# A fused attention and two-FFN kernel: the first stage's instructions put in an order written as a string, and x split by one operation per engine and tile

## The chip, the core and the metric

The kernel runs on one core of a Trainium2 chip. The metric is the device time of one execution in microseconds (us). The engines of the core are PE (matrix products, with its weight loads shown apart as PEld), DVE (vector), ACT (scalar functions), POOL (a second, slower vector engine) and SP, whose queue issues all the DMA transfers. Each engine takes its instructions strictly in the order in which the program has them; an instruction that waits holds up everything behind it on its engine.

## The reference, cut to what matters

```python
# q, k, v: (4, 8, 576, 64); chunks of 64 rows attend within themselves
scores = matmul(q_c, k_c.T) / 8
attn = exp(scores - max(scores)); attn /= sum(attn) + 1e-9
x = matmul(attn, v_c)  -> transposed to (2304, 512)
# first FFN: w_in (512, 2048), w_out (2048, 512), float64 in memory
h = x @ w_in
x = (h - tanh(h)) @ w_out
# second FFN: 8 experts (512 -> 1024 -> 512), weighted by a normalised gate
P = softmax-like matrix (2304, 8), rows and columns normalised 8 times
out = sum_e P[:, e:e+1] * (maximum(x @ w1[e], 0) @ w2[e])
```

## The kernel before

The 2304 tokens are 18 attention tiles of 128 rows (128 rows hold two chunks, and all 8 heads lie beside each other in 512 columns), and 6 blocks of 384 tokens for the FFNs; three tiles make a block. Every operand of an FFN product is kept as a high and a low part, and a product of two such operands is three PE products (`mm3`).

One attention tile T goes through: loads of q, k and v (three DMAs of 256 KB); four PE transposes each of q and k, copied out of PSUM by ACT (`stage_a`, L253 and L255); 16 small products for the scores into the one PSUM tile `s` (L265), then on DVE the row maximum and the subtraction (L268, L270) and on ACT the exponential (L271); the sum, the reciprocal and the scaling of the rows (`stage_b2`, L277 to L281: DVE for the first four tiles, then POOL scales); four transposes of the result, copied to the one tile `at` (`stage_c`, L288, L290); and 16 products with v into the one PSUM tile `x` (L300), which is split into x_hi (ACT, L307) and x_lo (DVE, L308), half a tile at a time (`stage_d`).

The first FFN is done in slots. Slot i makes one 128x384 piece of h from x and a quarter of w_in (12 PE products, L320, "h"; `layer1`), sends it through a polynomial and tanh on ACT, DVE and POOL in the slots that follow (`act_1`, `act_2`, `act_3a`, `act_3b`), and makes one piece of the second product, of a slot that is six back (12 PE products, L320, "y"; `layer2_ffn1`), which DVE adds to an accumulator (L398). 24 slots use one quarter of the weights; there are 96. The weights come from memory as 64-bit floats: `split64` takes a 128x512 piece apart with DVE bit operations (L160, L161), two ACT operations (L166, L167), two DVE operations (L169, L170), a POOL product (L171), and a high and a low part (ACT L174, POOL L175). 16 pieces are taken apart before slot 30.

In the stretch in which attention runs, the program emits its stages round by round (`ROUNDS`, `ROUND`), and a scheduler of the language then orders the instructions of each engine by its own rules. From `ctx.enter_context(tc.manual_schedule())` on, behind the last attention tile, the order is that of the code, slot by slot. What the second FFN does, behind slot 96, is written out by hand as well.

Of the kernel before, what the change touches and what calls it, by code (L numbers as in the profile page):

```python
# [8 lines left out]
F32 = mybir.dt.float32  # L9
# [3 lines left out]
ALU = mybir.AluOpType  # L13
# [14 lines left out]
def block_attention_two_ffn_kernel(ctx, tc, q, k, v, w_in, w_out, w_gate, w1, w2, out):  # L28
# [123 lines left out]
    def split64(key):  # L152

        which, u, c = key
        t = raws.pop(key).bitcast(U32).rearrange("p (n two) -> p n two", two=2)
        lw, hw = t[:, :, 0], t[:, :, 1]
        e = cvp.tile([P, 512], F32, tag="cve", name="cve")
        m = cvp.tile([P, 512], F32, tag="cvm", name="cvm", bufs=2)
        eu, mu = e.bitcast(U32), m.bitcast(U32)
        nc.vector.tensor_scalar(eu, hw, 20, 0x7FF, ALU.logical_shift_right, ALU.bitwise_and)  # L160
        nc.vector.tensor_scalar(mu, hw, 0xFFFFF, None, ALU.bitwise_and)  # L161
        if cvq:
            ep, mp = cvq[0].tile([P, 512], F32, tag="cvq", name="cvq"), pgp[0].tile([P, 512], F32, tag="sm", name="cvs")
# [12 lines left out]
        (w1t if which == "a" else w2t)[u, c] = (hi, lo)
# [16 lines left out]
    def do_load(n=1):  # L193
        for _ in range(n):
            if nload[0] < len(order):
                load_raw(order[nload[0]])
                nload[0] += 1

    running = []

    def split_step():

        if not running and nsplit[0] < NS64:
            running.append(split64(order[nsplit[0]]))
            nsplit[0] += 1
        if running:
            try:
                next(running[0])
            except StopIteration:
                running.pop()  # L210
                do_load()

    def early_step(n=1):
        for _ in range(n):
            if nsplit[0] < 10 or running:
                split_step()

    def next_raw(which, k):
        if k < NU2:
# [24 lines left out]
            )  # L244
        st[T][nm] = t

    def stage_a(T):
        r = st[T]
        for nm in ("q", "k"):
            pt = ps.tile([P, NP, P], F32, tag="t", name="t", bufs=2)  # L250
            src = r.pop(nm).rearrange("p (n two) d -> p n (two d)", two=2)
            for p in range(NP):
                nc.tensor.transpose(pt[:, p, :], src[:, p, :], ident)  # L253
            r[nm + "t"] = t = ap_.tile([P, NP, P], F32, tag=nm + "t", name=nm + "t")
            nc.scalar.copy(t, pt)  # L255

    def stage_b(T):
        r = st[T]
        qt, kt = r.pop("qt"), r.pop("kt")
        sp = ps.tile([P, NP, 2, CH], F32, tag="s", name="s")  # L260
        for p in range(NP):
            for c in range(2):
                for h in range(2):
                    hs, cs = slice(h * D, (h + 1) * D), slice(c * CH, (c + 1) * CH)
                    nc.tensor.matmul(sp[hs, p, c, :], qt[hs, p, cs], kt[hs, p, cs], start=True, stop=True)  # L265
        s3 = sp.rearrange("p n c j -> p (n c) j")
        mx = ap_.tile([P, 2 * NP], F32, tag="mx", name="mx")
        nc.vector.tensor_reduce(mx, s3, AX.X, ALU.max)  # L268
        ex = ap_.tile([P, 2 * NP, CH], F32, tag="ex", name="ex", bufs=3)
        nc.vector.tensor_tensor(ex, s3, mx.unsqueeze(2).to_broadcast([P, 2 * NP, CH]), ALU.subtract)  # L270
        nc.scalar.activation(ex, ex, AF.Exp, scale=1.0 / float(D) ** 0.5)  # L271
        r["ex"] = ex

    def stage_b2(T):
        ex = st[T]["ex"]
        sm = ap_.tile([P, 2 * NP], F32, tag="sm", name="sm")
        nc.vector.tensor_reduce(sm, ex, AX.X, ALU.add)  # L277
        nc.vector.tensor_scalar(sm, sm, EPS, None, ALU.add)
        nc.vector.reciprocal(sm, sm)
        eng = nc.vector if T < 4 else nc.gpsimd  # L280
        eng.tensor_tensor(ex, ex, sm.unsqueeze(2).to_broadcast([P, 2 * NP, CH]), ALU.mult)  # L281

    def stage_c(T):
        r = st[T]
        ex = r.pop("ex").rearrange("p (n c) j -> p n (c j)", c=2)
        pt = ps.tile([P, NP, P], F32, tag="t", name="t", bufs=2)
        for p in range(NP):
            nc.tensor.transpose(pt[:, p, :], ex[:, p, :], ident)  # L288
        r["at"] = at = ap_.tile([P, NP, P], F32, tag="at", name="at", bufs=1)
        nc.scalar.copy(at, pt)  # L290

    def stage_d(T):
        r = st.pop(T)
        at, vt = r["at"], r["v"]
        px = ps.tile([P, 2, 512], F32, tag="x", name="x")
        for p in range(NP):
            for c in range(2):
                for h in range(2):
                    hs, cs = slice(h * D, (h + 1) * D), slice(c * CH, (c + 1) * CH)
                    nc.tensor.matmul(  # L300
                        px[hs, c, p * CH:(p + 1) * CH], vt[cs, 2 * p + h, :], at[cs, p, hs], start=True, stop=True
                    )
        b, t = divmod(T, TT)
        for c in range(2):
            o = slice(t * P + c * CH, t * P + (c + 1) * CH)
            src = px[:, c, :NP * CH].rearrange("p (n i) -> p n i", n=NP)
            nc.scalar.copy(x_hi[b][:, :, o], src)  # L307
            nc.vector.tensor_tensor(x_lo[b][:, :, o], src, f(x_hi[b][:, :, o]), ALU.subtract)  # L308


    acc = {}
# [35 lines left out]
    def act_1(i, ph):  # L347
        z = tmp.tile([P, TB], F32, tag="z", name="z")
        t = tmp.tile([P, TB], F32, tag="t", name="t", bufs=2)
        s1 = tmp.tile([P, TB], F32, tag="s1", name="s1")  # L350
        if s2p:
            s2 = s2p[0].tile([P, 512], F32, tag="s2", name="s2p")[:, :TB]
        else:
            s2 = tmp.tile([P, TB], F32, tag="s2", name="s2", bufs=2)
# [710 lines left out]
        return i // SPU, i % SPU // 4, i % 4  # L1065

    nsteps = {}
    for r in range(6):
        nsteps[SPU - 6 + r] = nsteps[SPU + r] = 1 + (r % 2)
    for r in range(SPU + 6, NS1 - SPU + 6):  # L1070
        nsteps[r] = 2 if r == SPU + 21 else 1

# [10 lines left out]
    todo = {}  # L1083

    def slot(i):
        u, b, c = at(i)
        while u == 0 and ((u, c) not in w1t or i >= LAG and (u, 3) not in w2t):
            split_step()
        ph = layer1(*at(i))
        if nsteps.get(i, 0) > 1:  # L1090
            split_step()
# [7 lines left out]

    PRE = early
    ROUNDS = ("BAb", "BEAbE", "DCBbEAE", "ABbE")
    ROUND = "DCBSEbASE"
    stages = {"A": stage_a, "B": stage_b, "b": stage_b2, "C": stage_c, "D": stage_d}
    before = {"B": "A", "b": "B", "C": "b", "D": "C"}
    done = dict.fromkeys(stages, 0)
    i = r = 0
    load(0, "q", q)
    load(0, "k", k)  # L1110
    while done["D"] < NTILE:
        if r + 1 < NTILE:
            load(r + 1, "q", q)
            load(r + 1, "k", k)
        if 1 <= r <= NTILE:
            load(r - 1, "v", v)
        if r < 2:
            do_load()
        goal = r - 3 if r < 7 else r - 4 if r < 10 else r * 4 // 3 - 8
        for op in ROUNDS[r] if r < len(ROUNDS) else ROUND:  # L1120
            if op == "E":
                early_step()
            elif op == "S":
                if i < min(PRE, goal, 4 * (done["D"] // TT)):
                    slot(i)
                    i += 1
            elif done[op] < (done[before[op]] if op in before else min(NTILE, r + 1)):
                stages[op](done[op])
                done[op] += 1
        r += 1  # L1130
    assert i <= PRE
    actx.close()
    yx = ExitStack()
    for r in rings:
        if r.more:
            r.extend(first=r not in (php, pyp), within=yx if r is pyp else ctx)
    accp += [pool(f"acc{b}") for b in range(4, NB)]
    pgp.append(yx.enter_context(tc.tile_pool(name="pgp", bufs=1, space=PSUM)))
    s2x = ExitStack()
    s2p.append(s2x.enter_context(tc.tile_pool(name="s2p", bufs=1, space=PSUM)))  # L1140
    cvq.append(s2x.enter_context(tc.tile_pool(name="cvq", bufs=1, space=PSUM)))
    ctx.enter_context(tc.manual_schedule())
    last = NS1 - SPU
    put = lambda r, task: todo.setdefault(last + r, []).append(task)
    put(0, gate_load)
# [114 lines left out]
```

## Time and profile before

| | us |
|---|---|
| median of three timed runs | 1978.49 |
| lowest and highest of them | 1977.0, 1979.21 |
| the profiled execution: its own time | 1978.26 |
| the profiled execution: span from first to last instruction | 1976.5 |
| busy in the span: PE, DVE, POOL, ACT | 1938.1, 1576.1, 1399.5, 918.7 |

The busy time of PE is made of pipelined instructions, so that 98% of the span says that PE rarely stands, not that its every instruction is at its best. The change touches the first 220 us or so; behind them the two programs do the same.

### The profile page before, as it was taken

Reading aid. Unit: us, or ns where it says so; the run is one execution under the profiler, and the core shown is the slowest. Engines: PE = TensorE matmul, PEld = TensorE weight load, DVE = VectorE, ACT = ScalarE, POOL = GpSimd, SP = SyncE. Lnnn points to the kernel's source line nnn. Section 1 sums busy time; section 2 is a strip of 40 time slices with the busy share of each in tenths; the row PEclk is TensorE's granted clock in tenths of the full one; section 3 lists DMA queues with packets and bytes.
Section 4 is the critical chain, followed back from the end, with each engine's and each line's share of the span. In section 5 each row is a group of like instructions: output and inputs, shape, how many; then the busy total and the mean of one; then the engine's idle time right before and its main releaser. Section 6 shows DMA issues by size and latency. Waiting matters only on the chain.

```text
span 1976.5 us, 35597 instructions
## 1 busy us (share of the span) xinstructions
PE 1938.1 (98%) x11708; PEld 1853.5 (94%) x11708; DVE 1576.1 (80%) x2599; ACT 918.7 (46%) x2095; POOL 1399.5 (71%) x1419
## 2 busy tenths in 40 slices
PE   7899999999999999999999999999999999999999
PEld 5799999999888889898889999999999999999998
DVE  7987888777689887778876888888877887777777
ACT  6766777766544655555543223222234233232222
POOL 3645677667566766667757888878778887777775
PEclk9899999999999999999999999999999999999999
DMA  8631111110498788888889888888888867988883
GB/s 182 149 82 38 54 44 44 43 33 22 148 316 287 274 302 303 301 296 303 313 287 348 259 262 260 262 261 252 262 258 260 260 212 264 314 261 262 261 252 118
DMA packets 307702, 430.51 MB, mean 218 GB/s; under 512 B 81696, under 2 KB 135232, under 8 KB 307520
## 3 DMA queue, kind: packets, MB, share of 16 engines
q1 hardware_dynamic: 307520, 428.25, 66.9%
q8 instruction: 94, 1.54, 0.3%
q14 instruction: 88, 0.72, 0.1%
HBM read 304.89 MB, written 123.26 MB: 217 GB/s over the span
## 4 chain that ended last, share of the span: by engine, by line
PE 78%; DVE 5%; ACT 1%; issue 1%; DMA 1%; POOL 1%; SPq 0%; DVEq 0%; POOLq 0%; ACTq 0%
PE h L592 33%; PE y L751 23%; PE y L320 16%; PE h L320 5%; DVE gl L600 1%; DVE acc L628 0%; DVE cvm L441 0%; DVE x L628 0%; DVE s L517 0%; ACT gh L599 0%; DMA raw<-in_moe_w 0%; DVE pm L1033 0%; DMA w1d<-wa 0%; DMA wb<-in_moe_w 0%; PE y L990 0%
## 5 line engine op out<-in xcount | busy, mean ns | idle before, releaser
L592 PE MATMUL h<-x,wa 128*128 128x384 f32 x4032 | 792.0, 337 | 1.6 <-DVE t L657 1.3
L592 PEld LDWEIGHTS h<-x,wa 128*128 128x128 f32 x4032 | 707.9, 188 | 13.7 <-DVE t L657 1.6
L751 PE MATMUL y<-gh,wb 128*128 128x384 f32 x1764 | 521.5, 336 | 0.6 <-issue 0.2
L756 DVE TENSOR_TENSOR acc<-y,acc 128x768 f32<-128x768 f32 x367 | 349.1, 954 | 135.7 <-PE y L751 135.1
L180 POOL TENSOR_TENSOR gl<-cvm,gh 128x384 fp32r<-128x384 f32 x252 | 264.6, 1050 | 133.7 <-ACT gh L179 133.7
L751 PEld LDWEIGHTS y<-gh,wb 128*128 128x128 f32 x1764 | 325.2, 188 | 2.4 <-ACT gh L179 1.5
L751 PE MATMUL y<-gl,wb 128*128 128x384 f32 x882 | 296.4, 336 | 0.0
L179 ACT CAST gh<-cvm 128x384 fp32r<-128x384 f32 x252 | 129.8, 515 | 288.7 <-DVE cvm L796 162.3
L179 ACT CAST gh<-z 128x384 fp32r<-128x384 f32 x189 | 97.4, 515 | 352.1 <-POOL z L812 226.6
L320 PE MATMUL y<-wb,gh 128*128 128x512 f32 x776 | 243.5, 395 | 0.0
L180 POOL TENSOR_TENSOR gl<-z,gh 128x384 fp32r<-128x384 f32 x189 | 199.7, 1056 | 45.6 <-ACT gh L179 41.2
L320 PE MATMUL h<-x,wa 128*128 128x384 f32 x1152 | 222.0, 340 | 5.9 <-DVE s L375 5.9
L320 PE MATMUL y<-gh,wb 128*128 128x384 f32 x768 | 214.1, 340 | 4.8 <-POOL wb L175 2.6
L320 PEld LDWEIGHTS h<-x,wa 128*128 128x128 f32 x1152 | 200.1, 189 | 9.6 <-DVE s L375 8.4
L320 PEld LDWEIGHTS y<-wb,gh 128*128 128x128 f32 x776 | 143.9, 188 | 26.0 <-issue 0.4
L751 PEld LDWEIGHTS y<-gl,wb 128*128 128x128 f32 x882 | 165.8, 188 | 0.0
L366 POOL TENSOR_TENSOR s<-s,s 128x384 f32<-128x384 f32 x96 | 99.1, 1033 | 82.4 <-DVE s L365 74.0
L320 PE MATMUL y<-wb,gl 128*128 128x512 f32 x388 | 152.9, 394 | 0.0
L180 POOL TENSOR_TENSOR wa<-cvm,wa 128x256 fp32r<-128x256 f32 x128 | 100.0, 781 | 73.4 <-ACT wa L179 70.9
L320 PEld LDWEIGHTS y<-gh,wb 128*128 128x128 f32 x768 | 141.3, 189 | 8.1 <-POOL wb L175 3.4
L599 ACT ACTIVATE gh<-h 128x384 fp32r<-128x384 f32 x99 | 48.7, 492 | 190.9 <-DVE h L688 96.2
L320 PE MATMUL y<-gl,wb 128*128 128x384 f32 x384 | 129.6, 338 | 0.0
(208 smaller groups left out, 3233.9 us busy)
## 6 DMA issues: line engine op xcount, KB each, us to landing
wa<-w1d SPq DMA_DIRECT2D x448, 256.0 KB, 3.2
wb<-w2d SPq DMA_DIRECT2D x441, 256.0 KB, 3.3
w1d<-wa SPq DMA_DIRECT2D x224, 256.0 KB, 2.7
w2d<-wb SPq DMA_DIRECT2D x192, 256.0 KB, 4.2
raw<-in_moe_w SPq DMA_DIRECT2D x33, 512.0 KB, 4.5
wb<-in_moe_w SPq DMA_DIRECT2D x62, 256.0 KB, 5.0
raw<-in_moe_w_in SPq DMA_DIRECT2D x16, 512.0 KB, 3.8
raw<-in_moe_w_out SPq DMA_DIRECT2D x16, 512.0 KB, 3.8
```

The lines of the kernel that those rows point to most:

```text
L179: nc.scalar.copy(hi, src)
L180: nc.gpsimd.tensor_tensor(lo, src, f(hi), ALU.subtract)
L320: nc.tensor.matmul(ps, lhsT, rhs, start=(i == 0), stop=(i == n - 1))
L366: nc.gpsimd.tensor_tensor(s1, s1, w, ALU.mult)
L592: nc.tensor.matmul(ps, w[:, a, kk, :], b[:, kk, :], start=(i < 3 and kk == 0 and s == 0), stop=(kk == 1 and s == 2), skip_group_check=(i > ...
L599: nc.scalar.activation(hi, src, AF.Relu)
L600: nc.vector.scalar_tensor_tensor(lo, src, 0.0, f(hi), ALU.max, ALU.subtract)
L751: nc.tensor.matmul(y[:, c, :], w[:, a, c, :], b, start=(s == 0), stop=(s == 2))
L756: nc.vector.tensor_tensor(m, y, m, ALU.add)
```

## The change

The scheduler is switched off from the first attention tile on. The stages are cut into 17 kinds of pieces, each a letter, with four more letters for the loads, and a string of 433 letters (`ORDER`) gives the order in which the program emits them; the n-th occurrence of a letter is the n-th tile, weight piece or slot. 1, 2 and 3 load q, k and v, 0 loads a raw weight piece; Q and K are the transposes, S the scores, B maximum, subtraction and exponential, R the row sums and scaling, C the transposes of the result, D the products with v, X the split of x; c, d and e are the three parts of taking a weight piece apart; l is the h product of a slot, z, y, x and w are the four parts of its activation, and m the y product. The string ends where slot 29 would have ended, with 30 l, 24 m and 16 weight pieces done. Behind it the program goes on with slot 30 as before.

The split of x is now one operation of 128x512 on each of ACT and DVE in place of two of 128x256. No other instruction is added or left out.

```diff
+ORDER = (
+    "2110KQ2Q1c1S2KBQdS01KR2BceCS3R0KBDdXQeR23CSQKD3BcR2SXC1dKD0X2QCe1cl3210B3KSzdQRBlyReDxXC2zS1QBKcyRl3",
...
-    def stage_a(T):
+    def turn(T, nm):
...
-        b, t = divmod(T, TT)
-        for c in range(2):
-            o = slice(t * P + c * CH, t * P + (c + 1) * CH)
-            src = px[:, c, :NP * CH].rearrange("p (n i) -> p n i", n=NP)
-            nc.scalar.copy(x_hi[b][:, :, o], src)
-            nc.vector.tensor_tensor(x_lo[b][:, :, o], src, f(x_hi[b][:, :, o]), ALU.subtract)
+    def split_x(T):
+        px = st.pop(T)["x"]
+        b, t = divmod(T, TT)
+        o = slice(t * P, (t + 1) * P)
+        src = px[:, :, :NP * CH].rearrange("p c (n i) -> p c n i", n=NP)
+        hi, lo = (x[b][:, :, o].rearrange("p n (c i) -> p c n i", c=2) for x in (x_hi, x_lo))
+        nc.scalar.copy(hi, src)
+        nc.vector.tensor_tensor(lo, src, f(hi), ALU.subtract)
...
-    for r in range(6):
-        nsteps[SPU - 6 + r] = nsteps[SPU + r] = 1 + (r % 2)
...
+    stages = {
+        "1": lambda T: load(T, "q", q), "2": lambda T: load(T, "k", k), "3": lambda T: load(T, "v", v),
+        "0": lambda j: do_load(),
+        "Q": lambda T: turn(T, "q"), "K": lambda T: turn(T, "k"), "S": scores, "B": soft_a, "R": soft_b,
+        "C": turn_ex, "D": times_v, "X": split_x,
+        "c": lambda j: split_begin(), "d": lambda j: next(running[dn[0] - en[0]]), "e": lambda j: split_end(),
+        "l": lambda i: ph_of.update({i: layer1(*at(i))}), "z": act_0, "y": act_2, "x": act_3a,
+        "w": lambda i: act_3b(i, at(i)), "m": lambda i: layer2_ffn1(*at(i)),
+    }
...
+    for op in "".join(ORDER):
+        stages[op](done[op])
+        done[op] += 1
+        dn[0], en[0] = done["d"], done["e"]
+        if op == "X" and done[op] == NTILE:
+            end_attention()
```

The first place is PE ahead of the first h product. In the names, t is a transposed tile, s the scores, x the product with v, and h the piece of slot 0. Before:

```order
18 L253 MATMUL t<-ident,q 128x128 x4
19 L300 MATMUL x<-at,v 64x64 x16
20 L253 MATMUL t<-ident,k 128x128 x4
21 L288 MATMUL t<-ident,ex 128x128 x4
22 L265 MATMUL s<-kt,qt 64x64 x16
23 L300 MATMUL x<-at,v 64x64 x13
24 L253 MATMUL t<-ident,q 128x128 x4
25 L300 MATMUL x<-at,v 64x64 x3
26 L253 MATMUL t<-ident,k 128x128 x4
27 L288 MATMUL t<-ident,ex 128x128 x4
28 L265 MATMUL s<-kt,qt 64x64 x16
29 L320 MATMUL h_635<-x,wa_329 128x384 x2
```

Now:

```order
16 L269 MATMUL t<-ident,k 128x128 x4
17 L318 MATMUL x<-at,v 64x64 x16
18 L281 MATMUL s<-kt,qt 64x64 x16
19 L306 MATMUL t<-ident,ex 128x128 x4
20 L269 MATMUL t<-ident,k 128x128 x4
21 L318 MATMUL x<-at,v 64x64 x16
22 L269 MATMUL t<-ident,q 128x128 x4
23 L306 MATMUL t<-ident,ex 128x128 x4
24 L341 MATMUL h_592<-x,wa_338 128x384 x2
```

Before, the scheduler cut the 16 products with v into pieces around other work; now each piece stands whole. Ahead of the first h product both programs have six transposes of q and of k, four of the result and three products with v; before there are six score products, now five.

The second place is DVE around the first splits of x (the destination x is a part of x_lo). Before:

```order
21 L268 TENSOR_REDUCE mx<-s 128x8
22 L160 TENSOR_SCALAR cve<-raw 128x512
23 L270 TENSOR_TENSOR ex<-s,mx 128x512
24 L308 TENSOR_TENSOR x<-x 128x4x64
25 L161 TENSOR_SCALAR cvm<-raw 128x512
26 L170 SCALAR_TENSOR_TENSOR cve<-raw,cve 128x512
27 L277 TENSOR_REDUCE sm<-ex 128x8
28 L308 TENSOR_TENSOR x<-x 128x4x64
29 L278 TENSOR_SCALAR sm<-sm 128x8
```

Now:

```order
21 L178 SCALAR_TENSOR_TENSOR cvm<-raw,cvm 128x512
22 L179 SCALAR_TENSOR_TENSOR cve<-raw,cve 128x512
23 L329 TENSOR_TENSOR x<-x 128x2x4x64
24 L295 TENSOR_REDUCE sm<-ex 128x8
25 L296 TENSOR_SCALAR sm<-sm 128x8
26 L297 RECIPROCAL sm<-sm 128x8
27 L299 TENSOR_TENSOR ex<-ex,sm 128x512
28 L287 TENSOR_REDUCE mx<-s 128x8
29 L289 TENSOR_TENSOR ex<-s,mx 128x512
```

Two rows of a tile have become one, and the operations of a piece stand together, where before those of two or three pieces were mixed.

## Rows read from the trace of the kernel before

**Rows 1.** PE by time around slot 0, slot 18 and slot 29's end (start, us).
```profile
37.44 0.80 PE L320 MATMUL h<-x,wa 128*128 128x384 f32 x3
...
164.20 2.35 PE L320 MATMUL h<-x,wa 128*128 128x384 f32 x12
...
218.96 0.34 PE L320 MATMUL y<-gh,wb 128*128 128x384 f32 x1
```

**Rows 2.** Busy by stretch: PE, PEld, DVE, ACT, POOL, granted clock, DMA share, GB/s.
```profile
0.00:9.35 9.35, 5.00 (x44) 3.93 (x44) 0.00 (x0) 2.46 (x3) 0.70 (x6) 1.00 0.95 197
9.35:164.20 154.85, 134.75 (x1689) 119.19 (x1686) 130.72 (x250) 109.10 (x239) 76.35 (x68) 0.96 0.54 122
164.20:219.20 55.00, 51.23 (x294) 49.72 (x288) 44.44 (x79) 39.14 (x87) 35.91 (x32) 1.00 0.16 49
220.10:400.00 179.90, 179.32 (x1031) 178.58 (x1032) 146.41 (x277) 135.14 (x304) 126.76 (x117) 1.00 0.15 45
400.00:1976.00 1576.00, 1567.72 (x8663) 1502.11 (x8661) 1253.59 (x1994) 632.24 (x1462) 1159.34 (x1198) 1.00 0.76 253
```

**Rows 3.** PE by time in a steady round of one tile and one slot.
```profile
126.33 0.69 PE L300 MATMUL x<-at,v 64*64 64x64 f32 x32
...
127.54 1.15 PE L265 MATMUL s<-kt,qt 64*64 64x64 f32 x32
128.62 2.35 PE L320 MATMUL h<-x,wa 128*128 128x384 f32 x12
...
132.89 0.60 PE L253 MATMUL t<-ident,q 128*128 128x128 f32 x4
...
133.86 0.69 PE L300 MATMUL x<-at,v 64*64 64x64 f32 x32
```

**Rows 4.** Busy by stretch again, inside the attention stretch.
```profile
9.35:111.00 101.65, 83.69 (x1095) 71.74 (x1093) 91.73 (x172) 73.36 (x158) 53.51 (x46) 0.95 0.69 157
...
37.44:68.00 30.56, 26.88 (x376) 23.27 (x374) 30.01 (x58) 26.35 (x59) 18.97 (x17) 1.00 0.72 172
```

**Rows 5.** What PE waited for, 30 to 220 us: total, times, longest.
```profile
PE h L320 <- DVE s L375: 3.8, 4, 1.4
PE x L300 <- DVE x L308: 3.6, 3, 2.0
PE s L265 <- ACT kt L255: 3.0, 3, 1.5
```

**Rows 6.** PE by time around a long wait.
```profile
71.09 0.45 PE L300 MATMUL x<-at,v 64*64 64x64 f32 x14 [1.99 <-DVE x L308]
...
73.28 1.98 PE L265 MATMUL s<-kt,qt 64*64 64x64 f32 x32
```

**Rows 7.** DVE by line and shape, first 164.2 us: busy us, mean ns, idle.
```profile
L365 DVE SCALAR_TENSOR_TENSOR s<-s,z 128x384 f32<-128x384 f32 x18 | 16.5, 917 | 0.0
L308 DVE TENSOR_TENSOR x<-x 128x256 fp32r<-128x256 f32 x34 | 14.1, 415 | 2.9 <-ACT x L307 2.9
...
L270 DVE TENSOR_TENSOR ex<-s,mx 128x512 f32<-128x512 f32 x18 | 12.3, 681 | 0.1
L375 DVE COPY_PREDICATED s<-z,t 128x384 f32<-128x384 uint32 x17 | 11.7, 688 | 3.7 <-POOL s L366 3.6
L363 DVE SCALAR_TENSOR_TENSOR s<-s,h 128x384 f32<-128x384 f32 x18 | 9.8, 547 | 4.5 <-ACT s L357 4.2
...
L161 DVE TENSOR_SCALAR cvm<-raw 128x512 uint32<-128x512 uint32 x10 | 7.4, 742 | 0.0
...
L398 DVE COPY acc<-y 128x384 f32<-128x384 f32 x12 | 6.6, 551 | 3.8 <-PE y L320 3.6
```

**Rows 8.** Two DVE lines, first 220 us: shortest, median and longest in ns.
```profile
L161 DVE TENSOR_SCALAR cvm<-raw x16: 410/1053/1259, 9.7 to 216.3; 128x512 uint32<-128x512 uint32 x16
...
L365 DVE SCALAR_TENSOR_TENSOR s<-s,z x18: 502/1082/1522, 41.8 to 163.4; 128x384 f32<-128x384 f32 x18
L365 DVE SCALAR_TENSOR_TENSOR s<-s2p,z x10: 541/552/557, 171.9 to 214.5; 128x384 f32<-128x384 f32 x10
```

More of the change, by code (lines that the diff above doesn't have):

```diff
@@ L18 @@
 CH = 64
+ORDER = (
+    "2110KQ2Q1c1S2KBQdS01KR2BceCS3R0KBDdXQeR23CSQKD3BcR2SXC1dKD0X2QCe1cl3210B3KSzdQRBlyReDxXC2zS1QBKcyRl3",
+    "DS3xXwKQB2CS1zDCdRBylXxzeQ0K1lcQ2ywzDS03KdC1wBlcy2RSxXlez2KR0QBy1D3XCKS2dxQD2X1CKwlcQBdS1eQKeB3Rz2yD",
+    "S1XK1xxQ0mClwwzym3DRz1lxwXBcymx0Cw3Rz3SB2lyDwKRmXRz3xCywQSBmdDC2lxXzlcyKDeS3zwByClRXxdzmRQx0DX3Cylww",
+    "mzS3DBClyRxXmx0Dz3wwlyXzCymDlXlxxzwcyxmlzwd0yemlzxcmweydzwxylmmlzcyemxwdxzy0mxwlzcywlm0dezwymmxxl0ez",
+    "wclywdzxc0ylmzwdmxylemxelwzywzm0m",
+)
 TMAX = 0.625
@@ L161, in split64 @@
         nc.vector.tensor_scalar(mu, hw, 0xFFFFF, None, ALU.bitwise_and)
-        if cvq:
+        if late_split(key):
             ep, mp = cvq[0].tile([P, 512], F32, tag="cvq", name="cvq"), pgp[0].tile([P, 512], F32, tag="sm", name="cvs")
@@ L199, in block_attention_two_ffn_kernel, with split_begin, split_end @@
     running = []
-    def split_step():
[L203 to L216, printed above, removed]
+    late_split = lambda key: order.index(key) >= 10
+    def split_begin():
+        running.append(split64(order[nsplit[0]]))
+        nsplit[0] += 1
+        next(running[-1])
+    def split_end():
+        for _ in running.pop(0):
+            pass
+    def split_step():
+        if not running:
+            if nsplit[0] < NS64:
+                split_begin()
+                phase[0] = 1
+        elif phase[0] == 1:
+            next(running[0])
+            phase[0] = 2
+        else:
+            split_end()
+            do_load()
+    phase = [0]
     def next_raw(which, k):
@@ L245, in load, with scores @@
         st[T][nm] = t
-    def stage_a(T):
+    def turn(T, nm):
         r = st[T]
[L249 to L257, printed above, removed]
+        pt = ps.tile([P, NP, P], F32, tag="t", name="t", bufs=2)
+        src = r.pop(nm).rearrange("p (n two) d -> p n (two d)", two=2)
+        for p in range(NP):
+            nc.tensor.transpose(pt[:, p, :], src[:, p, :], ident)
+        r[nm + "t"] = t = ap_.tile([P, NP, P], F32, tag=nm + "t", name=nm + "t")
+        nc.scalar.copy(t, pt)
+    def scores(T):
         r = st[T]
         qt, kt = r.pop("qt"), r.pop("kt")
-        sp = ps.tile([P, NP, 2, CH], F32, tag="s", name="s")
+        r["s"] = sp = ps.tile([P, NP, 2, CH], F32, tag="s", name="s")
         for p in range(NP):
@@ L265, in stage_b, with soft_a, soft_b @@
                     nc.tensor.matmul(sp[hs, p, c, :], qt[hs, p, cs], kt[hs, p, cs], start=True, stop=True)
-        s3 = sp.rearrange("p n c j -> p (n c) j")
+    def soft_a(T):
+        r = st[T]
+        s3 = r.pop("s").rearrange("p n c j -> p (n c) j")
         mx = ap_.tile([P, 2 * NP], F32, tag="mx", name="mx")
         nc.vector.tensor_reduce(mx, s3, AX.X, ALU.max)
-        ex = ap_.tile([P, 2 * NP, CH], F32, tag="ex", name="ex", bufs=3)
+        r["ex"] = ex = ap_.tile([P, 2 * NP, CH], F32, tag="ex", name="ex", bufs=3)
         nc.vector.tensor_tensor(ex, s3, mx.unsqueeze(2).to_broadcast([P, 2 * NP, CH]), ALU.subtract)
         nc.scalar.activation(ex, ex, AF.Exp, scale=1.0 / float(D) ** 0.5)
-        r["ex"] = ex
-    def stage_b2(T):
+    def soft_b(T):
         ex = st[T]["ex"]
@@ L279, in stage_b2, with turn_ex @@
         nc.vector.reciprocal(sm, sm)
-        eng = nc.vector if T < 4 else nc.gpsimd
+        eng = nc.vector if T < NORM else nc.gpsimd
         eng.tensor_tensor(ex, ex, sm.unsqueeze(2).to_broadcast([P, 2 * NP, CH]), ALU.mult)
-    def stage_c(T):
+    def turn_ex(T):
         r = st[T]
@@ L290, in stage_c, with times_v @@
         nc.scalar.copy(at, pt)
[L292 to L295, printed above, removed]
+    def times_v(T):
+        r = st[T]
+        at, vt = r.pop("at"), r.pop("v")
+        r["x"] = px = ps.tile([P, 2, 512], F32, tag="x", name="x")
         for p in range(NP):
@@ L350, in act_1 @@
         s1 = tmp.tile([P, TB], F32, tag="s1", name="s1")
-        if s2p:
+        if i >= early:
             s2 = s2p[0].tile([P, 512], F32, tag="s2", name="s2p")[:, :TB]
@@ L1085, in slot @@
     def slot(i):
-        u, b, c = at(i)
-        while u == 0 and ((u, c) not in w1t or i >= LAG and (u, 3) not in w2t):
-            split_step()
         ph = layer1(*at(i))
@@ L1098, in slot @@
             layer2_ffn1(*at(i - LAG))
[L1102 to L1106, printed above, removed]
-    done = dict.fromkeys(stages, 0)
[L1108 to L1141, printed above, removed]
@@ L1142, in block_attention_two_ffn_kernel, with end_attention @@
-    ctx.enter_context(tc.manual_schedule())
+    def end_attention():
+        actx.close()
+        for r in rings:
+            if r.more:
+                r.extend(first=r not in (php, pyp), within=yx if r is pyp else ctx)
+        accp.extend(pool(f"acc{b}") for b in range(4, NB))
+        pgp.append(yx.enter_context(tc.tile_pool(name="pgp", bufs=1, space=PSUM)))
+        s2p.append(s2x.enter_context(tc.tile_pool(name="s2p", bufs=1, space=PSUM)))
+        cvq.append(s2x.enter_context(tc.tile_pool(name="cvq", bufs=1, space=PSUM)))
@@ new lines, in block_attention_two_ffn_kernel, with act_0 @@
+    NORM = 4
+    yx, s2x = ExitStack(), ExitStack()
+    ctx.enter_context(tc.manual_schedule())
+    ph_of = {}
+    def act_0(i):
+        act_1(i, ph_of.pop(i))
+    stages = {
[7 more added lines that the diff above has]
+    }
@@ L1143, in block_attention_two_ffn_kernel @@
+    done = dict.fromkeys(stages, 0)
+    dn, en = [0], [0]
+    for op in "".join(ORDER):
[4 more added lines that the diff above has]
+            end_attention()
+    i = done["l"]
     last = NS1 - SPU
```

## The prediction

> **What bounds the kernel now.** I read PE by time for the marks, then the busy times by stretch, then PE's waits, then DVE by line. Slot 0's h product starts at 37.44 us; the last tile's product with v is over when slot 18 starts at 164.20; the last of the 30 h and 24 y products that stand ahead of slot 30 begins at 218.96 and is over at about 219.2 [rows 1]. I call 9.35 to 164.2 stretch A and 164.2 to 219.2 stretch B. From 220 us on PE is busy for 179.3 of 179.9 and for 1567.7 of 1576 us [rows 2]; there the two programs are the same, so that part can only move forward as a whole, and what slot 30 wins the end wins.
>
> What PE needs is read in a steady round: from 126.33 to 133.86 us it does one tile, one h and one y product, 7.53 us; h and y are 128.62 to 132.89 of it, 4.27, so a tile is 3.26 us and a product of 12 about 2.1 [rows 3]. The 18 tiles, 18 h and 12 y of the time to 164.2 are 58.7 + 30 x 2.1 = 121.7 us. DVE needs more: it is busy for 130.7 of the 154.85 us of stretch A [rows 2], and it is the engine nearest to full. But it is full unevenly: 30.0 of 30.6 us between 37.4 and 68, yet 91.7 of 101.7 between 9.35 and 111 [rows 4]. PE's waits there are some 1 to 2 us each, on DVE and ACT, with no edge that stands out [rows 5]: the order is what costs. A long wait is followed by slow products: behind 1.99 us of idling at 71 us the scores of a tile took 1.98 us against 1.15 in the steady round [rows 6, 3]; the mean granted clock of stretch A is 0.96 [rows 2].
>
> **The change, part by part.** *DVE's work ahead of slot 18.* In the string 18 tiles, 18 h, 9 y products, 10 weight pieces, 17 letters y and 15 letters x stand ahead of the letter of slot 18. Against the counts of before [rows 7] that is three accumulator writes fewer (12 to 9, 0.55 each), one L363 and one L365 fewer with the subtraction that goes with them (0.55 + 0.92 + about 0.55) and two predicated copies fewer (17 to 15, 0.69 each): 5.0 us by duration. Neighbours on DVE overlap somewhat, so I take 4.5. This work moves into stretch B.
>
> *The split of x.* 36 DVE operations of 0.415 us become 18; 34 of the 36 lay in stretch A. The price of the new one is not in the trace. Bounds: 0.83 us, if nothing is saved, and 0.68, as L270, which also reads 512 columns from PSUM and writes as many [rows 7]. I take 0.68: 18 x 0.68 = 12.2 in place of 14.1, of which I count 0.5, since a split in two also overlaps with its neighbours; at the other bound it is 18 x 0.83 = 14.9, 0.8 lost. ACT's half of the edit lies under other work: ACT is busy for 109 of 155 us [rows 2]; without that cover it would be of the same size. Left: 130.7 - 4.5 - 0.5 = 125.7.
>
> *DVE waiting beside POOL.* L365 takes 0.55 us when an operand lies in PSUM (s2p) and up to 1.5 when all lie in SBUF; L161 takes 0.41 at best, 1.05 in the median [rows 8]. In stretch A the excess is 18 x (0.917 - 0.550) + 10 x (0.742 - 0.410) = 9.9 us [rows 7, 8]. POOL is busy for 76 of 155 us; over some 134 it would be 57% where it was 49%, so the excess may grow by a sixth. I add 2 (0 to 4, or the excess falls away): 127.7, say 128.
>
> The Trainium skill ("SBUF — State Buffer", section "SBUF: two separate sides") says that DVE and GpSimd share one port pair, that whoever starts first holds it for a whole instruction, and that the other blocks fully. The trace agrees: the form of L365 with a PSUM operand never passes 0.557 us, the SBUF form reaches 1.522. It speaks against the change: by it, packing both engines more densely costs DVE time.
>
> *Where DVE starts.* The first raw weight piece is now the fourth transfer on SP's queue, behind three loads of 256 KB; before it was the fifth, and DVE started at 9.35. At the 197 GB/s of that time [rows 2] one load less is 1.3 us: 8.1.
>
> *How full DVE gets* decides. Bounds from before: 0.90 (9.35 to 111 us) and 0.98 (37.4 to 68) [rows 4]. I followed the string by hand up to slot 0, with slow score products of 1.98 us and DVE pieces of 0.68: the weight piece starts at 8.1, the first scores end near 9.5, and from there nearly every DVE piece finds its operand ready, down to the third X at about 31 us, where before slot 0 came at 37.4. Further on the one PSUM tile each for s and x makes PE wait for a DVE piece that stands just ahead in the string, and such waits come back to DVE. I take 0.95: 128 / 0.95 = 134.7, so slot 18 starts at 8.1 + 134.7 = 142.8. PE allows it with 58.7 + 27 x 2.1 = 115.4 us of work.
>
> *Stretch B.* 12 h and 15 y products of 2.08 us are 56.2. Before, 24 products took 55.0, so 5.1 us were waits, mostly of h for the predicated copy L375 [rows 1, 5]. DVE has 44.4 + 4.5 = 48.9 us of work here, under 0.87 of the time. I take 2 us of waits (0 to 5): 58.2.
>
> *Sum.* 142.8 + 58.2 = 201.0 against 219.2: 18.2 us less. The profiled execution took 1978.26 us, its span 1976.5, and the median of the runs is 0.23 above it: 1978.26 - 18.2 = 1960.1. By the bounds: 8.1 + 128 / 0.98 + 56.2 = 194.9, which gives 1954; 8.1 + 128 / 0.90 + 61.3 = 211.6, which gives 1971. DMA is covered: its share over stretch A is 0.54 [rows 2]; without that cover it would be v that comes late, for the product with v.
>
> **The rivals.** *DVE's excess beside POOL falls away.* If the string keeps the two engines' SBUF work apart, DVE needs 128 - 12 = 116 us, and PE bounds: at slot 0 (31 us) it has done about 15 of its 115.4 us, so slot 18 comes at 131.4 and the end of stretch B at 188 to 189: 30.5 us less, 1948. For it: the 0.41 us at best show that it happens [rows 8]. Against it: POOL is busy half the time, and an order fixed in advance does not place to a fraction of a microsecond.
>
> *The string's own waits replace the scheduler's.* There is one PSUM tile x, so the split of tile T stands between two products with v. If PE waits 1 us more there, then DVE for its operands, 18 tiles give 18 us back: 1978, no change. For it: the engines keep strict order, and this edge has a wait of 2.0 us before. Against it: it cost 3.6 us in all [rows 5].
>
> *PE falls to 1.2 GHz.* Products behind a long wait took nearly twice as long [rows 6]. From slot 0 at 31 us to slot 18 at 142.8 PE has 111.8 us for 100.4 of work, 11.4 to spare. To end over 4 us later than before it must lose 11.4 + 18.2 + 4 = 33.6 us, that is stay at the lower level for 67 of these 112 us; at 75 us it gives 1986. Against it: before, stretch A lost 154.85 x 0.04 = 6.2 us [rows 2], 12.4 us at that level, a fifth of it. For it: a string in strict order can idle PE once a tile.
>
> **How the numbers follow.** The forecast, 1954 to 1971, has 0.66; PE as the bound, 1948, 0.14; waits replaced, 1974.5 to 1982, 0.09; the lower clock, 1983 and more, 0.11. 0.2%, 4 us, is about what a measurement of this kernel can tell from no change. Faster: the first two, 0.80; within 4 us 0.09; slower 0.11. The range from 1947 to 1974 holds the first two and leaves out 2 in 10.
>
> **What would show it.** In the changed kernel: DVE starts near 8 us; slot 0 near 31; slot 18 near 143, with DVE busy for about 128 of the 135 us between; the y product ahead of slot 30 is over near 201; the time from there to the end is as before; the split of x on DVE takes 0.68 us. The forecast is wrong if DVE is less than 0.9 full ahead of slot 18, if L365's SBUF form comes to 0.55 or over 1.1 us in the mean, or if the granted clock of stretch A is under 0.9.

## The result and the profile after

The changed kernel takes 1953.18 us (median of four runs, 1951.67 to 1953.81) where the kernel before takes 1978.85 (median of four runs on the same chip): a ratio of 0.9871, 95% interval 0.9854 to 0.9888, 25.7 us less. The forecast was 1960.1, 18.2 us less. The whole range, 1947 to 1974, held the time; the range of the likeliest case, 1954 to 1971, missed it by 0.8 us. The profiled execution took 1951.67 us with a span of 1949.9, 26.6 us under the span of before.

All of it is won ahead of slot 30. PE by time in the changed kernel, at the marks of [rows 1]: slot 0 starts at 29.30 us, and the last y product ahead of slot 30 begins at 192.53, with slot 30 right behind it.

```profile
29.30 0.42 PE L341 MATMUL h<-x,wa 128*128 128x384 f32 x1
...
192.53 0.34 PE L341 MATMUL y<-gh,wb 128*128 128x384 f32 x1
192.70 1.03 PE L341 MATMUL h<-x,wa 128*128 128x384 f32 x5
```

Busy times by stretch of the changed kernel, columns as in [rows 2]. The cuts are DVE's start (8.10), slot 0 (29.30), the middle, slot 18 (136.54) and slot 30 (192.70); the last two lines answer to the last two of [rows 2].

```profile
8.10:136.54 128.44, 117.80 (x1674) 106.23 (x1671) 117.97 (x229) 102.02 (x217) 73.70 (x65) 1.00 0.68 149
...
29.30:78.00 48.70, 43.88 (x674) 38.50 (x673) 45.77 (x87) 41.94 (x88) 30.12 (x27) 1.00 0.83 181
78.00:136.54 58.54, 58.07 (x716) 54.73 (x709) 52.47 (x106) 45.91 (x103) 37.95 (x35) 1.00 0.38 91
136.54:192.70 56.16, 56.16 (x325) 56.16 (x325) 43.20 (x86) 42.36 (x96) 41.14 (x38) 1.00 0.18 57
192.70:372.60 179.90, 179.38 (x1035) 179.06 (x1035) 143.31 (x275) 132.24 (x302) 122.93 (x114) 1.00 0.13 42
372.60:1949.90 1577.30, 1567.74 (x8660) 1501.42 (x8658) 1254.62 (x1993) 630.42 (x1461) 1158.07 (x1198) 1.00 0.77 253
```

Three things are to be read here. From 78 us on PE no longer stands: 58.07 of 58.54 us, then 56.16 of 56.16. The granted clock of the attention stretch is 1.00, where it was 0.96 [rows 2]. And from the end of the last y product ahead of slot 30 to the end of the program it is 1757.2 us, as it was before (1757.3, from 219.2 us), so nothing is given back.

What PE still waits for between 29 and 230 us is short (total, times, longest); the edges of [rows 5] have all but gone:

```profile
PE s L281 <- DVE ex L289: 1.5, 3, 1.0
PE h L341 <- DVE t L389: 1.4, 1, 1.4
PE t L306 <- ACT kt L271: 0.8, 1, 0.8
```

Where the time came from is read on PE. Up to 219.2 us PE was busy for 190.97 us and stood for 28.2; up to 192.70 it is busy for 177.82, with the same 2016 products, and stands for 14.9. So 13.2 of the 26.5 us are the same products done in less busy time, and 13.3 are waits gone. Of the first, at most 6.2 us answer to the granted clock (0.04 of the 154.85 us of stretch A before). Another part lies at the start, where products are slow in both kernels, but for longer before. Transposes of q and of k in the kernel before:

```profile
20.92 1.03 PE L253 MATMUL t<-ident,q 128*128 128x128 f32 x4
...
22.14 0.66 PE L253 MATMUL t<-ident,k 128*128 128x128 f32 x4
```

In the changed kernel the last slow ones take 0.98 us at 10.60. PE is busy for 12.04 of the first 21.5 us before and for 6.95 of the first 11.3 now. The same scores take 1.98 us slow and 1.15 fast (the last section has the rows), so the 5.09 us of difference are worth about 2.1 us, an estimate from these rows. What made up the other 5 us or so is not shown.

DVE by line and shape to slot 18 (busy us, mean ns, idle ahead of it), to be held against [rows 7]. L386 is the L365 of before, L170 the L161, L396 the L375, L329 the L308.

```profile
L329 DVE TENSOR_TENSOR x<-x 128x512 fp32r<-128x512 f32 x18 | 12.2, 679 | 0.8 <-ACT x L328 0.8
...
L386 DVE SCALAR_TENSOR_TENSOR s<-s,z 128x384 f32<-128x384 f32 x17 | 11.2, 658 | 0.0
L396 DVE COPY_PREDICATED s<-z,t 128x384 f32<-128x384 uint32 x17 | 10.2, 614 | 0.4 <-POOL s L387 0.3
...
L384 DVE SCALAR_TENSOR_TENSOR s<-s,h 128x384 f32<-128x384 f32 x17 | 9.3, 549 | 3.8 <-ACT s L378 3.7
L179 DVE SCALAR_TENSOR_TENSOR cve<-raw,cve 128x512 uint32<-128x512 uint32 x10 | 7.6, 764 | 0.0
...
L296 DVE TENSOR_SCALAR sm<-sm 128x8 f32<-128x8 f32 x18 | 6.9, 385 | 0.6
...
L169 DVE TENSOR_SCALAR cve<-raw 128x512 uint32<-128x512 uint32 x10 | 4.4, 439 | 9.7 <-DMA raw<-in_moe_w_in 8.1 <-POOL cvm L180 1.5
L170 DVE TENSOR_SCALAR cvm<-raw 128x512 uint32<-128x512 uint32 x10 | 4.2, 420 | 0.0
...
L299 DVE TENSOR_TENSOR ex<-ex,sm 128x512 f32<-128x512 f32 x4 | 2.8, 692 | 0.1
```

L299 and L296 are the L281 and L278 of the kernel before, which had them so:

```profile
L281 DVE TENSOR_TENSOR ex<-ex,sm 128x512 f32<-128x512 f32 x4 | 4.9, 1217 | 0.1
L278 DVE TENSOR_SCALAR sm<-sm 128x8 f32<-128x8 f32 x18 | 3.8, 208 | 0.2
```

Most operations with all operands in SBUF have become shorter: 917 to 658 ns, 742 to 420, 688 to 614, 1217 to 692. Two of them have become longer: L296, from 208 to 385 ns, and L179, the L170 of before, from 721 to 764. L384, the L363 of before, which has an operand in PSUM, has stayed: 547 and 549 ns.

### The profile page after: what moved, and what is told of

It is laid out like the page before. It is cut to its first block, busy times and chain, and to the rows that moved or that the text cites. A ratio compares the mean times of both kernels' runs of the same rounds, so it can differ in the third digit from the quotient of the medians.

```text
span 1949.9 us, 35582 instructions
## 1 busy us (share of the span) xinstructions
PE 1924.9 (99%) x11708; PEld 1845.7 (95%) x11708; DVE 1559.1 (80%) x2581; ACT 910.1 (47%) x2077; POOL 1396.5 (72%) x1419
## 4 chain that ended last, share of the span: by engine, by line
PE 77%; DVE 7%; ACT 1%; issue 1%; POOL 1%; DMA 0%; DVEq 0%; POOLq 0%; ACTq 0%
PE h L613 32%; PE y L772 23%; PE y L341 16%; PE h L341 5%; DVE gl L621 1%; DVE acc L649 1%; DVE cvm L462 0%; DVE x L649 0%; ACT gh L620 0%; DVE acc L652 0%; DVE s L538 0%; DMA raw<-in_moe_w 0%; DVE pm L1054 0%; DVE h L709 0%; PE y L1011 0%
```

## The experiments

All medians; the ratio is to the kernel before on the same chip, with its 95% interval. The kernel before is at 1.0, the changed kernel at 0.9871. Differences in us between two runs are often between two chips, on which the kernel before has medians of 1978.85 to 1979.81; they are good to about 1 us.

### The string with the old split of x

```diff
-        nc.scalar.copy(hi, src)
-        nc.vector.tensor_tensor(lo, src, f(hi), ALU.subtract)
+        for c in range(2):
+            o = slice(t * P + c * CH, t * P + (c + 1) * CH)
+            src = px[:, c, :NP * CH].rearrange("p (n i) -> p n i", n=NP)
+            nc.scalar.copy(x_hi[b][:, :, o], src)
+            nc.vector.tensor_tensor(x_lo[b][:, :, o], src, f(x_hi[b][:, :, o]), ALU.subtract)
```

> The changed kernel with the old split of x (two operations of 128x256 per tile on ACT and on DVE). If DVE bounds the time ahead of slot 18, its 36 operations of 0.415 us in place of 18 of 0.68 lengthen DVE's work by up to 2.7 us and the kernel by 1.5 to 2.7 us (1954.7 to 1956). If PE bounds it from 78 us on, as its busy share of 58.07 in 58.54 us there says, only the tiles ahead of 78 us count, under 1 us: 1953 to 1954.

Measured: 1965.18 us, 0.9927 (0.9914 to 0.9939). 12 us are lost, where 0 to 3 were expected from the lengths of the operations. ACT by time, then DVE by time, around one split (a bracket is the idle time ahead of an operation and what ended it):

```profile
46.74 0.41 ACT L328 CAST x<-x 128x256 fp32r<-128x256 f32 x1
...
48.73 0.37 ACT L328 CAST x<-x 128x256 fp32r<-128x256 f32 x1 [1.58 <-DVE x L329]
```

```profile
48.29 0.41 DVE L329 TENSOR_TENSOR x<-x 128x256 fp32r<-128x256 f32 x1
...
49.13 0.42 DVE L329 TENSOR_TENSOR x<-x 128x256 fp32r<-128x256 f32 x1 [0.44 <-ACT x L328]
```

ACT has its first half done at 47.15 and does nothing until DVE's first half, which only starts at 48.29, is over; then DVE stands while ACT does the second. The numbers themselves do not ask for ACT's wait, since its second half touches other columns than DVE's first half; why the program has it is not shown here. The waits of ACT and of DVE in this kernel, to slot 30, say that it is so in every tile:

```profile
ACT x L328 <- DVE x L329: 17.6, 18, 1.6
```

```profile
DVE x L329 <- ACT x L328: 7.9, 18, 0.4
```

ACT's standing is handed on, since its copies of the transposes come late. This is what PE waits for between 29 and 205 us:

```profile
PE t L306 <- ACT kt L271: 5.3, 3, 2.4
PE x L318 <- DVE x L329: 3.6, 3, 1.6
```

and by stretch PE does less work at a lower clock in the middle of the attention:

```profile
29.30:78.00 48.70, 40.48 (x620) 36.01 (x621) 42.75 (x85) 38.38 (x86) 26.86 (x24) 0.96 0.73 162
```

The clock does not account for the loss. The profiled execution reads 0.998 over the whole program and took 1964.8 us; two others of the five read 1.000 and took 1966.23 and 1965.18.

### Two halves, ACT's first

```diff
+        for c in range(2):
+            nc.scalar.copy(x_hi[b][:, :, o[c]], src[c])
+        for c in range(2):
+            nc.vector.tensor_tensor(x_lo[b][:, :, o[c]], src[c], f(x_hi[b][:, :, o[c]]), ALU.subtract)
```

> The changed kernel with x split in two halves again, but both ACT halves ahead of both DVE halves. With ACT and DVE in turn, ACT's second half waited for DVE's first in all 18 tiles (17.6 us) and DVE's second for ACT's second (7.9 us), and the kernel took 1965. If that waiting in turn is the loss, it goes here and only the extra operations stay (2.2 us of ACT, 2.7 of DVE): 1953 to 1957. If the number and length of the operations is the loss, 1963 to 1966.

Measured: 1952.98 us, 0.9869 (0.9853 to 0.9886), as the changed kernel. The number of operations is that of the run above, the order on each engine another, and the whole 12 us are back. In this kernel ACT waits for DVE's part of the split in no tile. The loss was the waiting in turn, not the length or the number of the operations.

### The one operation alone, in the kernel before

```diff
-        for c in range(2):
-            o = slice(t * P + c * CH, t * P + (c + 1) * CH)
...
+        nc.scalar.copy(hi, src)
+        nc.vector.tensor_tensor(lo, src, f(hi), ALU.subtract)
```

> The kernel before, scheduler and all, with x split by one operation per engine and tile. If waiting in turn is what the one operation takes away, the scheduler, which put other work between the halves (waits of 5.5 us on ACT and 2.9 on DVE), gains less than the string does: 1973 to 1978. If the two edits add up, 1967 (11 to 12 us less).

Measured: 1980.96 us, 1.0006 (0.9997 to 1.0016): no change, outside what either theory said. So the two edits do not add up: the split is worth nothing without the string and 12 us with it. The rows of before fit this. There the scheduler put other DVE operations between the halves of a split (three at the place shown with the change), and ACT's wait for a split, to 219 us, was a third of what it is with the string:

```profile
ACT x L307 <- DVE x L308: 5.5, 7, 1.3
```

### The string, ordered again by the scheduler

The line that switches the scheduler off moves from ahead of the loop over the string into `end_attention`, behind the last attention tile, where it stood before.

```diff
         cvq.append(s2x.enter_context(tc.tile_pool(name="cvq", bufs=1, space=PSUM)))
+        ctx.enter_context(tc.manual_schedule())
 
     NORM = 4
     yx, s2x = ExitStack(), ExitStack()
-    ctx.enter_context(tc.manual_schedule())
```

> The same string, but the scheduler may reorder what it emits up to the last split of x; behind it strict order as in the changed kernel. If the gain is in the strict order of the string, most of what stretch A won (some 21 us) goes: 1968 to 1975. If the gain is in the pieces, in the earlier loads and in the stretch behind slot 18, it stays: 1953 to 1958.

Measured: 1963.27 us, 0.9918 (0.9904 to 0.9932), between what the two theories said. Slot 0 starts at 34.7 us, slot 18 at 149.2, slot 30 at 205.4. The order in which the program is emitted, pieces and one split included, is worth 16 us even if the scheduler rearranges it; that it is kept strictly is worth 10 more. Busy between the same cuts as above:

```profile
29.30:78.00 48.70, 42.79 (x614) 37.29 (x611) 43.22 (x80) 39.15 (x81) 27.75 (x24) 0.93 0.71 165
```

### The order of before, kept strictly

```diff
     done = dict.fromkeys(stages, 0)
     i = r = 0
+    ctx.enter_context(tc.manual_schedule())
     load(0, "q", q)
```

> The kernel before with the scheduler off from the start, so that each engine has the rounds of the code as they are written. If strict order alone were the gain, about 1960. If it is this string, the rounds stand no better than what the scheduler made of them: 1985 to 2020.

Measured: 2006.8 us, 1.0138 (1.0123 to 1.0153), slower. Strictness by itself is no gain; with the order in which the rounds are written PE waits for ACT, 16.2 us in seven waits. Busy from 8.1 us to slot 18, and the largest item of PE's waits there:

```profile
8.10:193.00 184.90, 145.43 (x1709) 130.90 (x1705) 137.33 (x247) 109.97 (x238) 74.42 (x67) 0.87 0.46 104
```

```profile
PE t L288 <- ACT qt L255: 16.2, 7, 4.1
```

The clock is 0.87 there: up to 0.13 of 184.9 us, 24 us, is lost to it, so this run also shows what the third rival (PE at 1.2 GHz) looks like.

### The string's tail in the order of the slots

```diff
-    "mzS3DBClyRxXmx0Dz3wwlyXzCymDlXlxxzwcyxmlzwd0yemlzxcmweydzwxylmmlzcyemxwdxzy0mxwlzcywlm0dezwymmxxl0ez",
+    "mzS3DBClyRxXmx0Dz3wwlyXzCymDlXxwzemmmlxyzwcmldxyzwe0mlxyzwcmldxyzwe0mlxyzwcmldxyzwe0mlxyzwcmldxyzwe0",
```

> The string up to the last split of x as it is, and behind it the slot order of the kernel before (h, parts of a weight piece, activation parts, y), with three y products moved ahead to reach the same state. If the string's order behind slot 18 is worth what the waits of the kernel before were, 3 to 5 us are lost: 1956 to 1958. If PE is full there whatever the order, 1953.

Measured: 1959.43 us, 0.9896 (0.9883 to 0.991); 6.2 us are lost, more than either theory gave. The same letters behind the last X, in the order of the slots before, end at 199.95 instead of 192.70. Of these 7.3 us of the profiled execution, 1.4 are there at slot 12 already (107.97 against 106.58), where the two programs are still the same. Busy of that part, and PE's largest wait in it:

```profile
137.00:199.00 62.00, 58.23 (x331) 56.79 (x329) 47.68 (x84) 41.36 (x92) 38.31 (x34) 1.00 0.14 43
```

```profile
PE h L341 <- DVE s L396: 4.6, 5, 1.4
```

This is the first edge of [rows 5], back with 4.6 us where it had 3.8.

### All row scaling on DVE, and all of it on POOL

```diff
-    NORM = 4
+    NORM = NTILE
```

```diff
-    NORM = 4
+    NORM = 0
```

> The scaling of the softmax rows is done by DVE for all 18 tiles (before: for 4, then POOL): 14 x 0.69 = 9.7 us more work for DVE ahead of slot 18, 15.6 us less for POOL. If DVE bounds that stretch, 8 to 10 us are lost: 1961 to 1963. If PE bounds it from 78 us on and DVE has some 10 us to spare (it is busy for 118 of 128 us), 1 to 5 us: 1954 to 1958.

> The scaling of the softmax rows is done by POOL for all 18 tiles, the first four too: 4 x 0.69 = 2.8 us less for DVE ahead of slot 0, 4.4 us more for POOL, and 0.4 us longer for the chain of each of these tiles. If DVE's work bounds the start, 2 to 3 us are won: 1950.5 to 1951. If the chain from the scores to the next product bounds it, or DVE's wait for POOL, 0 to 6 us are lost: 1953 to 1959.

Measured: with 14 more scalings on DVE 1964.8 us, 0.9924 (0.9908 to 0.9939); with all on POOL 1952.93, 0.9866 (0.9851 to 0.9881), no change. The 14 operations are 9.7 us by the length of L299, and 11.6 are lost: slot 4 comes 4.9 us later than in the changed kernel, slot 8 6.4, slot 12 8.7 and slot 18 11.9. The delay grows over the whole stretch, also where PE had no idle time to lose. Busy by stretch with all on DVE:

```profile
8.10:148.40 140.30, 120.89 (x1676) 109.01 (x1673) 130.72 (x243) 102.82 (x217) 58.69 (x51) 0.96 0.61 137
...
78.00:136.54 58.54, 54.10 (x680) 50.33 (x679) 54.01 (x104) 43.01 (x94) 27.88 (x25) 1.00 0.46 110
```

The clock of 0.96 does not explain it: an execution that reads 1.000 over the whole program took 1965.35 us, as long as the rest. DVE is 0.93 full here, and more work on it costs more than its length; 2.8 us taken off it at the start (NORM = 0) give nothing. So from 78 us on PE and DVE are both near their limit, and the string has no room for more DVE work.

### A weight piece's first DVE operations moved

The first DVE operations of weight pieces 5 to 10 (the letters c, L169 and L170) stand in the string, five of the six, one to three letters ahead of a letter y, whose POOL operations follow. These five are put behind that y, by 1 to 3 letters. In a second kernel all six are put behind the next B or X, by 2 to 12 letters (the expectations have 1 to 8 and 1 to 10). The eighth piece has no y near it; it is moved by the same 2 letters, behind a B, in both kernels. One of the three lines of the string that differ in the first of the two:

```diff
-    "DS3xXwKQB2CS1zDCdRBylXxzeQ0K1lcQ2ywzDS03KdC1wBlcy2RSxXlez2KR0QBy1D3XCKS2dxQD2X1CKwlcQBdS1eQKeB3Rz2yD",
+    "DS3xXwKQB2CS1zDCdRBylXxzeQ0K1lQ2ycwzDS03KdC1wBlyc2RSxXlez2KR0QBy1D3XCKS2dxQD2X1CKwlQBcdS1eQKeB3Rz2yD",
```

> The string with the first part c of the weight pieces 5 to 10 moved behind the next letter y (by 1 to 8 letters), where POOL is just busy with that y's product of 1.0 us. If DVE waits for POOL's running instruction, the first of c's two operations grows from 0.44 to some 0.9 us in these six, and the kernel loses 2 to 6 us: 1955 to 1959. If not, 0.4 us stays and the time is 1953 to 1954.

> The control to the run with c behind y: the first part of the weight pieces 5 to 10 is moved by 1 to 10 letters here too, at least as far, but behind the next B or X, where in the string it mostly stands and POOL is less often busy. If the loss of 10 us behind y came from waiting for POOL, the first of c's operations stays near 0.45 us here and the loss is 0 to 5 us: 1953 to 1958. If it came from moving the piece at all (its later parts find no slack), about 1963 again.

Measured: behind y 1963.25 us, 0.9924 (0.9909 to 0.9939); behind the next B or X 1961.24, 0.9913 (0.9898 to 0.9928). L169 by its shortest, median and longest, over all 16 pieces, first in the changed kernel, then with c behind y:

```profile
L169 DVE TENSOR_SCALAR cve<-raw x16: 406/427/1017, 8.1 to 180.6; 128x512 uint32<-128x512 uint32 x16
```

```profile
L169 DVE TENSOR_SCALAR cve<-raw x16: 417/746/1132, 8.2 to 193.9; 128x512 uint32<-128x512 uint32 x16
```

The six moved operations take 0.98, 1.13, 0.76, 0.85, 1.04 and 1.04 us where they took 0.59, 0.41, 0.43, 0.43, 0.42 and 0.43. A DVE operation on SBUF does wait for a POOL operation that has begun: 3.1 us in sum. The first of the six begins 0.31 us after one of POOL and ends 0.29 us after it:

```profile
44.17 1.00 POOL L387 TENSOR_TENSOR s<-s,s 128x384 f32<-128x384 f32 x1 [0.78 <-DVE s L386]
```

```profile
44.48 0.98 DVE L169 TENSOR_SCALAR cve<-raw 128x512 uint32<-128x512 uint32 x1
```

The Trainium skill ("SBUF — State Buffer", section "SBUF: two separate sides") says that the one that comes second blocks until the other's instruction is over, and these rows agree. But the loss is 10 us, and the second kernel, which was meant as the control, lost 8, with 1.5 us of such waiting (0.66, 1.13, 0.67, 0.86, 0.42 and 0.42 us). The second operation of these pieces, L170, adds to both: two took 1.23 and 1.24 us behind y, and two 1.23 and 1.27 in the second kernel, where all took 0.42, so that the sums are about 4.7 and 3.1 us. In the second kernel c came close to its own d, twice so that DVE waited for ACT between them; its DVE waits and its busy time show this and the cost on PE:

```profile
DVE cvm L178 <- ACT cvm L176: 5.8, 2, 3.4
```

```profile
29.30:78.00 48.70, 41.94 (x590) 38.03 (x589) 42.96 (x79) 37.92 (x80) 27.64 (x24) 0.89 0.70 156
```

The clock of 0.89 over 48.7 us is at most 5.4 of the 8 us; another execution of this kernel, which reads 0.998 over the whole program where the profiled one reads 0.996, took the same 1960.86 us. So the pair does not weigh the waiting beside POOL by itself: both displacements cost 8 to 10 us, each with waits of its own, and how much of it the waiting beside POOL is stays open.

### PE warmed up

Ten transposes of the identity, which nothing reads, are put ahead of all other work on PE.

```diff
+    warm = ps.tile([P, NP, P], F32, tag="s", name="s")
+    for p in range(10):
+        nc.tensor.transpose(warm[:, p % NP, :], ident, ident)
```

> Ten transposes of the identity, whose result nothing reads, ahead of everything else on PE, which waits until 4.03 us for the first k. If the slow products at the start (1.97 us for the first scores against 1.15) follow from what PE did before, the first transposes and scores run faster and slot 0 comes 0.5 to 1 us earlier: 1952 to 1953. If PE is simply slow at a program's start, or if the start waits for DMA anyway, nothing changes: 1953 to 1954.

Measured: 1951.72 us, 0.9861 (0.9845 to 0.9878): no gain that can be told from the changed kernel. PE by time at its start:

```profile
1.36 2.40 PE L1148 MATMUL s<-ident 128*128 128x128 f32 x10 [1.36 <-POOL ident masks.py:199]
...
6.89 1.15 PE L281 MATMUL s<-kt,qt 64*64 64x64 f32 x32
...
9.10 0.63 PE L269 MATMUL t<-ident,k 128*128 128x128 f32 x4 [1.06 <-DMA k<-in_k]
```

The first scores take 1.15 us, at 6.89, but the k of the next tile is then waited for, and slot 0 comes at 29.8, half a microsecond later than without.

## Why the prediction was right, point by point

**The start was as predicted.** DVE starts at 8.10 us (8.1 forecast), slot 0 at 29.30 (31). The string keeps DVE supplied from the first weight piece on.

**DVE's work ahead of slot 18: the direction was right, one term had the wrong sign.** Forecast 128 us, measured 117.97. By durations the sum of the operations fell by 16.1 us: 3.1 by five operations that now stand behind slot 18 (three accumulator writes, one L363, one L365), 1.9 by the split, and the rest, about 11, is what is left when some operations became shorter and two longer. (The two predicated copies that I had also moved are still ahead of it.) I had added 2 us for waiting beside POOL. In the trace the waiting fell on balance: L365 917 to 658 ns, L161 742 to 420, and the four scalings by DVE 1217 to 692. That is the first rival's mechanism, to which I gave 0.14 because an order fixed in advance would not keep the two engines apart. It does, for the weight pieces almost wholly and for L386 by two thirds of its excess over 0.55.

**How full DVE gets: forecast 0.95, measured 0.92** (117.97 of 128.44). This is 4.3 us the other way: 118 / 0.95 = 124.2. The two errors together put slot 18 at 136.54 in place of 142.8, 6.3 us earlier.

**PE as the bound.** The rival had slot 18 at 131.4. From 78 us on it holds: PE is busy for 58.07 of 58.54 us. But it idles for 4.8 of the 48.7 us between slot 0 and 78, and its work came to 102 us from slot 0 where 100.4 had been worked out; slot 0 was 1.7 us earlier, and 131.4 - 1.7 + 1.6 + 4.8 + 0.5 is the 136.6 measured. The result lies between my likeliest case and this rival, 0.8 us below the likeliest's own range, and it is nearer to the rival. That DVE bounds alone was wrong, but that it has slack would be wrong too: added DVE work came back with 11.6 us for 9.7.

**What was luck.** The likeliest case had DVE as the bound, with 128 us of work at 0.95. That work was 10 us too much, worth 10.5 us at 0.95, and the lower fullness took 4.3 of them back; two errors of opposite sign kept the time near that case. The range held it because the range also took in the rival with PE as the bound. The sum also priced the split and the order each for itself, where the runs show that they hang together: 12 us for the split with the string, nothing without it.

**Stretch B: forecast 58.2, measured 56.16**, the lower bound: no wait is left, where I had taken 2 us.

**The granted clock** was a term that I had only as a danger. At most 6.2 us lay in the 0.96 of before, and the profiled execution of the changed kernel reads 1.00: I had counted them nowhere, since a stretch bounded by DVE would not have gained by them. In the five runs that lose 8 us or more against the changed kernel with the string in place, the stretch from 29.3 to 78 us reads 0.89 to 0.96 instead of 1.00. But it reads 0.96 too with all scaling on POOL, which loses nothing, and the losses of the old split and of the scaling on DVE stand in executions that read 1.000 as well. So the clock goes along with the waits, and what it is worth by itself is not shown.

**The split of x** was priced by the length of its operations, 0.68 us for one and 0.5 gained in all. The length is right (679 ns). The price was wrong in kind: with strict order the old split is a wait of ACT for DVE and of DVE for ACT in each of 18 tiles, and 12 of the 25.7 us hang on it.

**The other rivals.** PE's wait for the split of x, which was to give all back, is 0.3 us in all in the changed kernel. It is 3.6 us with the old split. The fall to 1.2 GHz did not come; the rounds of before in strict order show it at 0.87, so it was a real danger, and the string, with its shorter waits, mostly kept it away (0.998 to 1.000 over the whole program in its four executions).

None of the three signs came that would have made the forecast wrong: DVE is over 0.9 full, the SBUF form of L365 lies between 0.55 and 1.1 us, and the clock is 1.00.

**What stays open.** How the 26 us divide among waits beside POOL, ACT and DVE in turn and the clock, and what made PE's products some 5 us shorter beyond the clock and the start. The parts do not add (12 for the split and 10 for the strict order in the string, nothing and -28 without it), and the control for POOL brought a wait of its own.

## What to carry to other kernels

Where two engines share a tile's work in halves and the order is strict, write all of the first engine's halves, then the second's, or use one operation: in turn, each waits for the other, which no duration shows. Price an order by the waits that it makes in its stretch rather than by sums of durations, and look at PE's busy time too: half of this gain was the same products done in less of it. Do not put a loss down to the granted clock of one execution: here it differed between executions of the same instructions. When two edits come together, run each alone both in the old kernel and in the new one; here one was worth nothing in the first and 12 us in the second.

## What was not expected of the hardware

In the first microseconds the products run at about half rate while the granted clock reads 1.00 for that stretch too. PE by time in the changed kernel: the same scores of a tile take 1.98 us at 7.42 and 1.15 at 11.51; with ten transposes ahead of them the first took 1.15 as well.

```profile
7.42 1.98 PE L281 MATMUL s<-kt,qt 64*64 64x64 f32 x32
...
11.51 1.15 PE L281 MATMUL s<-kt,qt 64*64 64x64 f32 x32
```

The 1.00 is no measurement there: the records of the granted clock in the traces begin at 21.7 us in the kernel before, at 11.3 in the changed kernel and at 5.7 with the ten transposes, and time without a record counts as 1.00. The products become fast just there: between 20.92 and 22.14 us before, between 10.60 and 11.51 now.

Waits of PE and a lower granted clock are seen side by side, and no run sets one apart. In the string with two halves, with the scheduler, and with c behind the next B, PE's longest wait between slot 0 and slot 30 is 2.4 to 3.1 us, and the clock from 29.3 to 78 us is 0.89 to 0.96; in the changed kernel the longest is 1.4 us, and the clock 1.00. Yet the clock is also 0.93 with a longest wait of 1.8 us (scaling on DVE) and 0.96 with 1.0 us (on POOL) and 1.4 us (tail in slot order). In the last of these the program is that of the changed kernel up to slot 18, and PE waits 0.75 and 1.04 us in the same place, ahead of the products at 46.43 and 48.10 us (45.45 and 47.12 in the changed kernel). Behind these waits the clock falls to the lower of its two levels, 1.2 GHz, in the one execution and stays at 2.4 GHz in the other. The four transposes that follow, with the tail in slot order, then in the changed kernel:

```profile
50.26 1.11 PE L306 MATMUL t<-ident,ex 128*128 128x128 f32 x4
```

```profile
48.85 0.66 PE L306 MATMUL t<-ident,ex 128*128 128x128 f32 x4
```

A second DVE operation that stands directly behind the first never had to wait for POOL in the changed kernel, though the first sometimes did:

```profile
L170 DVE TENSOR_SCALAR cvm<-raw x16: 412/420/423, 8.4 to 181.0; 128x512 uint32<-128x512 uint32 x16
```

That is no rule. With c behind y, two of these operations took 1.23 and 1.24 us, where POOL had begun its next operation while the first one on DVE was still running:

```profile
L170 DVE TENSOR_SCALAR cvm<-raw x16: 413/418/1239, 8.5 to 194.3; 128x512 uint32<-128x512 uint32 x16
```
